# A kernel ordered by its own planner: transfers planned as two first-in first-out queues, hand-over margins changed

## The chip, the cores and the metric

The kernel runs on one core of a Trainium2 chip. The time is device microseconds of that core; the engines are named as the profile names them: PE (matrix multiply, PEld its weight loads), DVE, ACT, POOL, and SP, which here only issues transfers (DMA).

## The reference

```python
# q, k, v: (4, 8, 576, 64); windowed attention, heads 0-3 plain window 32, heads 4-7 dilated by 4
scores = np.where(masks[None], scale * np.matmul(q, k.transpose(0, 1, 3, 2)), -1e9)
attn = softmax(scores)                                   # over the last axis
x = np.matmul(attn, v) -> tokens x heads: (2304, 512)
g = x @ w_gate                                           # 512 -> 1536
x = (g * (1.0 / (1.0 + np.exp(-g))) * (x @ w_val)) @ w_out   # 1536 -> 512
h = x @ w_in                                             # 512 -> 2048
out = (h - np.tanh(h)) @ w2_out                          # 2048 -> 512
```

All in float32. The weights reach the kernel as 64-bit floats, viewed as integers.

## The kernel before, in words

**Work.** 48 attention units (a pair of heads, 192 query rows) come first. The 2304 tokens are six tiles of 384, in three pairs. Layer 1 (gate, value, out) and layer 2 (in, out) go over blocks of 128 hidden columns, one or two blocks to a *turn*: seven turns in layer 1, eight in layer 2, each over the three pairs of tiles. Every matmul product is made of float32r high and low halves. Where a turn has two blocks and a pair of tiles is joined, the four products of a layer's first matrix are made from seven (`seven_up`), with sums of tiles (`sums_x`) and of weights (`sums_w`) made beforehand.

**Names of the steps.** `convert` brings a weight piece: a transfer into one of two staging buffers `st` (L262), then on ACT `rebias` (L265), which waits for the transfer, on DVE `shift`, `low_bits`, `sign` (L269, L273, L278), the last reader of the staging buffer, then the split into halves (ACT L247, DVE L250). In `seven_up` PE makes products (L429), ACT moves partial sums between PSUM banks (`seed` L440, `keep` L466), DVE adds (L469, L472). The second matrix of layer 1 is L610, of layer 2 L630; ACT or DVE take its result to an accumulator tile `acc` (`put`, L574, L570, L572), and a whole `acc` tile is stored, by SP the first time (L593), by POOL with an accumulating transfer later (L595), and fetched back once for the last turn (L558). Sums of tiles that don't stay on the core are stored (L658) and loaded again (L673). PSUM has 8 banks `ps`.

**What sets the order.** Each step is a task with an engine, a duration, a priority, what it depends on and what buffers it takes. `Plan.order` plays the tasks through in a list of events: whenever an engine is free it takes the ready task with the smallest priority number for which buffers are free. A task is ready a margin after the last task it depends on has ended: `NEAR` on the same engine, `FAR` from another one, or the margin `lat` that the earlier task carries. Tasks are then issued in the order of their planned starts, and on the chip each engine runs its own list strictly in that order, SP its transfers as well: one that has to wait holds up all behind it.

A transfer is, in the plan of before, a task of an engine "DMA" with a fixed duration, one after the other, and a fixed margin behind it. An accumulating store is a POOL task and then an empty "DMA" task of 3.8 us.

Of the kernel before, what the change touches and what calls it, by code (L numbers as in the profile page):

```python
# [23 lines left out]
DM = H * D  # L24
# [63 lines left out]


class Task:  # L90
    def __init__(self, n, eng, dur, prio, emit, deps, bufs, gives, lat, port):
        self.lat, self.n, self.eng, self.dur, self.prio, self.emit = lat, n, eng, dur, prio, emit
        self.port = port
        self.deps, self.bufs, self.gives = [d for d in deps if d is not None], list(bufs), gives
        self.then, self.ready, self.start, self.left = [], 0.0, None, len(self.deps)


class Plan:
# [2 lines left out]
    def __init__(self, rings):  # L101
        self.tasks, self.free = [], {r: list(range(n)) for r, n in rings.items()}

    def add(self, eng, dur, prio, emit, deps=(), bufs=(), gives=None, lat=None, port=False):
        t = Task(len(self.tasks), eng, dur, prio, emit, deps, bufs, gives, lat, port)
        for b in t.bufs:
            b.users += 1
        self.tasks.append(t)
        return t

    def order(self):
        for t in self.tasks:
            for d in t.deps:
                d.then.append(t)
        busy = dict.fromkeys(self.ENGINES, 0.0)
        waiting = {e: [t for t in self.tasks if t.eng == e and not t.left] for e in self.ENGINES}
        events, done, now = [], [], 0.0
        port = None, 0.0
        while True:
            moved = True  # L120
            while moved:
                moved = False
                for e in self.ENGINES:
                    if busy[e] > now:
                        continue
                    best = None
                    for t in waiting[e]:
                        if t.ready > now + 1e-9 or (best is not None and (t.prio, t.n) >= (best.prio, best.n)):
                            continue
# [22 lines left out]
            now, _, t = heapq.heappop(events)  # L152
            if t is None:
                continue
            for u in t.then:
                u.left -= 1
                u.ready = max(u.ready, now + (t.lat or (NEAR if u.eng == t.eng else FAR)))
                if not u.left:
                    waiting[u.eng].append(u)
                    heapq.heappush(events, (u.ready, -1, None))  # L160
# [34 lines left out]
def attention_then_two_ffns(ctx, tc, qk, vt, masks, w1, w2, out):  # L195
# [59 lines left out]
    def convert(src, prio, first=False):  # L255
# [33 lines left out]
    def sums_w(c1, c2, prio):  # L289
# [11 lines left out]
        a = plan.add("DVE", 1.4, prio, combine, [d1, d2], [u1, u2], port=True)  # L301
        return split_w(u1, [a], prio), split_w(u2, [a], prio)


# [28 lines left out]
    def attention(b, hp, g, prio, evac_on):  # L333
# [50 lines left out]
        a = add_att("DMA", Q_DMA, prio, lambda: nc.sync.dma_start(out=q(), in_=qk[b, hp, g]), bufs=[q], lat=DMA_FAR)  # L384
        got_v = add_att("DMA", V_DMA, prio, lambda: nc.sync.dma_start(out=v(), in_=vt[b, hp, g]), bufs=[v], lat=DMA_FAR)
# [167 lines left out]
    def add_up(layer, t, pieces, first, last, prio, early=None):  # L553
# [1 line left out]
        at = new_acc()  # L555
        keep = sums[layer - 1][t]
        if last:
            fetched = plan.add("DMA", 2.0, prio - 6.0, lambda: nc.sync.dma_start(out=at(), in_=keep),  # L558
                               [sum_done[t], early or pieces[0][4][0]], [at], lat=5.0)
        puts = []  # L560
        for n, (mm, c0, c1, dur, deps, bufs) in enumerate(pieces):
            ps = new_ps()
# [32 lines left out]
                nc.gpsimd.dma_start(out=keep, in_=at(), accum_op=ALU.add)  # L595

        if first:
            sum_done[t] = plan.add("DMA", 2.1, prio - 5.0, store, puts, [at], lat=5.0)
# [21 lines left out]
    def ffn2_out(ws, ys, t, first, last, prio, end=False, early=None):  # L620
# [17 lines left out]
        if last:  # L638
            at, puts = r
            for (s, c0, c1), a in zip(cuts, puts):  # L640
                def store(s=s, c0=c0, c1=c1):
                    r0 = t * TT + s * P
                    nc.sync.dma_start(out=out[r0:r0 + P, c0:c1], in_=at()[:, s * DM + c0:s * DM + c1])

                plan.add("DMA", 0.75 * (c1 - c0) / DM, -1e6, store, [a], [at])


    seven_x, spilled, fetched_x = {}, {}, {}
# [1 line left out]
    def spill(p, parts, prio):  # L650

        seven_x[p], spilled[p] = parts[:5], []
        for o, done in parts[5:]:
# [6 lines left out]
            spilled[p].append((home, plan.add("DMA", 2.0, prio, store, [done], [o], lat=4.5)))  # L660
        fetched_x.pop(p, None)

    homes = []
# [1 line left out]
    def parts_of(p, again, prio, begun):  # L665

        if not again or p not in fetched_x:
            fetched_x[p] = []
            for home, done in spilled[p]:
                o = new_x()  # L670

                def load(o=o, home=home):
                    nc.sync.dma_start(out=o().bitcast(F32).rearrange("p s k n -> p (s k n)"), in_=home)  # L673

                fetched_x[p].append((o, plan.add("DMA", 2.0, prio, load, [done, begun], [o], lat=4.5)))
        return seven_x[p] + fetched_x[p]

    def halves(r):
# [54 lines left out]
    def load_mask():  # L733
        nc.sync.dma_start(out=mask, in_=masks)

    got_mask = add_att("DMA", 1.0, ATT0 + 0.1, load_mask, lat=DMA_FAR)
    ps_warm = new_ps()

    def warm_up():
# [250 lines left out]
```

## Time and profile before

| | us |
|---|---|
| median of 3 runs (lowest, highest) | 910.91 (909.21, 913.83) |
| time of the profiled execution | 915.47 |
| its span, first to last instruction | 913.7 |
| PE busy in it | 891.1 |
| DVE, ACT busy in it | 657.6, 557.9 |

The profiled execution is one run, 4.56 us above the median; its span is 1.8 us shorter than its time. A matmul's busy time overlaps the next one's, so busy PE says that PE had no gap, not that it ran at its best.

### The profile page before, as it was taken

The page shows a single profiled execution, that of the slowest core. Times are in us where ns is not written, and L with a number is a line of the kernel's source. Part 1 is how long each engine was busy: PE and PEld are TensorE (multiplying, and loading weights), DVE is VectorE, ACT ScalarE, POOL GpSimd, SP SyncE. Part 2 cuts the span into 40 slices and gives each one's busy share as a digit, 9 for nine tenths or more (in the row PEclk, how much of TensorE's full clock was granted, in tenths as well). Part 3 has the DMA queues.
Part 4 walks back from the last instruction along what each step waited for, and adds up shares of the span by engine and source line. Part 5 has one row for each costly group of instructions (what it writes and reads, how often), then busy time and mean ns, then how long its engine had stood idle before and what let it go on. Part 6 is the DMA issues. An engine that isn't in the chain of part 4 may idle for free.

```text
span 913.7 us, 15222 instructions
## 1 busy us (share of the span) xinstructions
PE 891.1 (98%) x5322; PEld 839.5 (92%) x5322; DVE 657.6 (72%) x1573; ACT 557.9 (61%) x1461; POOL 92.4 (10%) x122
## 2 busy tenths in 40 slices
PE   8899999999999999999999999999999999999997
PEld 6789999999999999999999997988899989899986
DVE  4878897985644743753755999997786868775665
ACT  5688875856655654654655876775575656555531
POOL 2232310100000000000000000001010111111100
PEclk7799999999999999999999999999999999999999
DMA  9777844995675685586595566689889797959995
GB/s 277 216 244 259 281 125 121 250 316 151 176 197 105 173 206 106 130 221 168 129 281 178 197 241 253 229 233 236 222 216 239 179 236 188 238 114 228 254 268 219
DMA packets 48086, 189.60 MB, mean 208 GB/s; under 512 B 5504, under 2 KB 10368, under 8 KB 48000
## 3 DMA queue, kind: packets, MB, share of 16 engines
q1 hardware_dynamic: 38496, 136.63, 43.5%
q0 software_dynamic: 9504, 51.91, 31.3%
q8 instruction: 44, 0.72, 0.3%
q14 instruction: 42, 0.34, 0.1%
HBM read 113.02 MB, written 75.50 MB: 206 GB/s over the span
## 4 chain that ended last, share of the span: by engine, by line
PE 86%; DVE 6%; DMA 6%; issue 1%; ACT 1%; SPq 0%; ACTq 0%; DVEq 0%
PE ps L429 37%; PE ps L630 20%; PE ps L610 14%; PE ps L417 8%; PE ps L343 3%; DMA st<-w 3%; PE ps L381 2%; DMA q<-qk 2%; PE ps L368 2%; DVE x L688 1%; DVE y L496 1%; DVE acc L703 1%; DMA x<-part 1%; DVE u L278 0%; DVE wc L250 0%
## 5 line engine op out<-in xcount | busy, mean ns | idle before, releaser
L429 PE MATMUL ps<-x,wc 128*128 128x384 f32 x2184 | 399.5, 336 | 2.5 <-ACT acc L574 1.4
L429 PEld LDWEIGHTS ps<-x,wc 128*128 128x128 f32 x2184 | 383.3, 188 | 8.3 <-ACT ps L440 1.8
L630 PE MATMUL ps<-wc,y 128*128 128x512 f32 (+1 forms) x870 | 207.6, 390 | 0.1
L630 PEld LDWEIGHTS ps<-wc,y 128*128 128x128 f32 x870 | 161.8, 188 | 32.0 <-DVE t L541 0.6
L574 ACT ACTIVATE acc<-ps 128x384 f32<-128x384 f32 (+1 forms) x246 | 125.4, 528 | 91.0 <-PE ps L610 57.5
L610 PE MATMUL ps<-y,wc 128*128 128x384 f32 x864 | 163.4, 338 | 6.0 <-ACT acc L574 6.0
L610 PEld LDWEIGHTS ps<-y,wc 128*128 128x128 f32 x864 | 151.1, 188 | 7.3 <-ACT acc L574 7.3
L595 POOL DMA_DIRECT2D sum<-acc x66 | 57.5, 872 | 679.1 <-ACT acc L574 423.6
L496 DVE TENSOR_TENSOR y<-t,y 128x384 fp32r<-128x384 f32 x168 | 92.5, 555 | 26.7 <-ACT y L493 26.0
L247 ACT ACTIVATE wc<-u 128x512 fp32r<-128x512 f32 x104 | 65.4, 631 | 61.0 <-PE ps L429 43.4
L493 ACT ACTIVATE y<-t 128x384 fp32r<-128x384 f32 x168 | 87.0, 519 | 23.3 <-PE ps L630 12.1
L250 DVE TENSOR_TENSOR wc<-u,wc 128x512 fp32r<-128x512 f32 x104 | 71.7, 694 | 23.2 <-ACT wc L247 22.4
L469 DVE TENSOR_TENSOR ps<-ps,t 128x384 f32<-128x384 f32 x52 | 29.5, 566 | 69.3 <-PE ps L429 69.1
L417 PE MATMUL ps<-x,wc 128*128 128x384 f32 x384 | 72.0, 342 | 0.0
L417 PEld LDWEIGHTS ps<-x,wc 128*128 128x128 f32 x384 | 67.6, 192 | 0.3
L440 ACT ACTIVATE ps<-ps 128x384 f32<-128x384 f32 x104 | 49.7, 478 | 28.1 <-PE ps L429 26.4
L538 DVE SCALAR_TENSOR_TENSOR t<-t 128x384 f32<-128x384 f32 x96 | 53.2, 556 | 12.8 <-ACT t L535 12.4
L354 ACT ACTIVATE e<-e,nm 128x96 f32<-128x96 f32 x144 | 52.2, 371 | 11.3 <-DVE nm L348 11.3
L265 ACT ACTIVATE u<-st 128x512 f32<-128x512 f32 x68 | 45.1, 670 | 22.2 <-DMA st<-w 21.8
L535 ACT ACTIVATE t<-ps 128x384 f32<-128x384 f32 x72 | 35.2, 489 | 31.5 <-DVE ps L469 20.9
L343 PE MATMUL ps<-q 128*128 128x96 f32 x288 | 44.5, 302 | 4.4 <-DMA q<-qk 4.4
L269 DVE TENSOR_SCALAR u<-u 128x512 uint32<-128x512 uint32 x68 | 29.3, 432 | 26.6 <-ACT u L265 26.5
(61 smaller groups left out, 814.8 us busy)
## 6 DMA issues: line engine op xcount, KB each, us to landing
sum<-acc POOLq DMA_DIRECT2D x66, 768.0 KB, 8.4
x<-part SPq DMA_DIRECT2D x58, 768.0 KB, 6.3
st<-w SPq DMA_DIRECT2D x68, 512.0 KB, 5.6
q<-qk SPq DMA_DIRECT2D x48, 304.0 KB, 5.2
sum<-acc SPq DMA_DIRECT2D x12, 768.0 KB, 5.2
part<-x SPq DMA_DIRECT2D x12, 768.0 KB, 4.6
acc<-sum SPq DMA_DIRECT2D x12, 768.0 KB, 6.7
v<-vt SPq DMA_DIRECT2D x48, 144.0 KB, 4.2
```

Source lines behind the costliest of these rows:

```text
L247: nc.scalar.activation(out=w()[:, 0, :], in_=u(), func=AF.Copy)
L250: nc.vector.tensor_tensor(out=w()[:, 1, :], in0=u(), in1=w()[:, 0, :].bitcast(F32), op=ALU.subtract)
L343: nc.tensor.matmul(ps()[:, i * KT:(i + 1) * KT], lhsT=q()[:, i * P:(i + 1) * P], rhs=q()[:, k0:k0 + KT], start=True, stop=True)
L417: nc.tensor.matmul(ps()[:, :TT], lhsT=w()[:, a, kc * P:(kc + 1) * P], rhs=xt[kc // 2]()[:, bb, kc % 2, :], start=(n == 0), stop=(n == 3 * ...
L429: nc.tensor.matmul(ps()[:, :TT], lhsT=w()[:, i, c:c + P], rhs=b()[:, j, k, :], start=(start and n == 0), stop=(n == 5), skip_group_check=True)
L493: nc.scalar.activation(out=y()[:, 0, :], in_=s(), func=AF.Copy)
L496: nc.vector.tensor_tensor(out=y()[:, 1, :], in0=s(), in1=y()[:, 0, :].bitcast(F32), op=ALU.subtract)
L538: nc.vector.scalar_tensor_tensor(out=sq(), in0=sq(), scalar=E0 / E1, in1=sq(), op0=ALU.add, op1=ALU.mult)
L574: nc.scalar.activation(out=o, in_=ps()[:, :c1 - c0], func=AF.Copy)
L595: nc.gpsimd.dma_start(out=keep, in_=at(), accum_op=ALU.add)
L610: nc.tensor.matmul(ps()[:, :TT], lhsT=w[2][0]()[:, a, m * P:(m + 1) * P], rhs=y[0]()[:, bb, :], start=(start and n == 0), stop=(n == 3 * l ...
L630: nc.tensor.matmul(ps()[:, :c1 - c0], lhsT=y[0]()[:, a, s * P:(s + 1) * P], rhs=w[1][0]()[:, bb, c0:c1], start=(n == 0), stop=(n == 3 * le ...
```

## The change

Transfers get two first-in first-out queues in the plan: one for those that SP issues, one for those of POOL. SP is busy for `ISSUE`; the transfer enters its queue `LAUNCH` later; the head of each queue is worked on, alone at full rate, and when both queues have one at the rates of `DMA_SHARE`; it is done `LAND` after its work is used up. What depends on it follows `NEAR` after that in the attention part and `SLACK` after it elsewhere. The margins `FAR`, `FIRST_FAR`, `ATT_FAR`, `QUICK` and the priorities `CONV0` and `HURRY` have new values. No arithmetic, no buffer and no instruction's shape changes; every engine's list is ordered anew.

```diff
-    def add(self, eng, dur, prio, emit, deps=(), bufs=(), gives=None, lat=None, port=False):
+    def add(self, eng, dur, prio, emit, deps=(), bufs=(), gives=None, lat=None, port=False, work=0.0):
...
+    def rates(self, queues):
+        heads = [e for e in queues if queues[e]]
+        return [queues[e] for e in heads], [DMA_SHARE[e] for e in heads] if len(heads) > 1 else [1.0]
...
+        queues, moves = {"DMA": [], "POOL": []}, [0.0]
...
-                    heapq.heappush(events, (busy[e], best.n, best))
+                    heapq.heappush(events, (busy[e], best.n, best, "issued" if best.work else "done"))
...
+            if what == "issued":
+                heapq.heappush(events, (now + LAUNCH, t.n, t, "enter"))
+                continue
+            if what in ("enter", "moved"):
+                heads, rate = self.rates(queues)
+                for q, r in zip(heads, rate):
+                    q[0][0] -= (now - moves[-1]) * r
+                for q in heads:
+                    if q[0][0] < 1e-6:
+                        u = q.pop(0)[1]
+                        heapq.heappush(events, (now + LAND, u.n, u, "done"))
+                if what == "enter":
+                    queues[t.eng].append([t.work, t])
...
-NEAR, FAR = 0.2, 1.1
-FIRST_FAR, ATT_FAR, DMA_FAR = 0.2, 0.8, 1.8
+NEAR, FAR = 0.2, 0.7
+FIRST_FAR, ATT_FAR = 0.3, 0.5
+ISSUE, LAUNCH, LAND = 0.45, 1.1, 0.7
+DMA_SHARE = {"DMA": 0.4, "POOL": 0.6}
...
-CONV0 = -18.6
+CONV0 = -15.0
...
-SUM_DMA = 3.8
-Q_DMA, V_DMA = 1.02, 0.5
-QUICK = 0.6
-HURRY = 60.0
+SLACK = 1.5
+SUM_DMA = 3.9
+Q_DMA, V_DMA = 1.12, 0.5
+QUICK = 0.5
+HURRY = 20.0
...
-        a = plan.add("DMA", 1.5, prio, load, bufs=[st], lat=DMA_FAR if first else 3.0)
+        a = plan.add("DMA", ISSUE, prio, load, bufs=[st], lat=NEAR if first else SLACK, work=1.65)
...
-            a = plan.add("POOL", 0.62, prio - 5.0, store, puts + [sum_done[t]], [at], lat=2.0)
-            sum_done[t] = plan.add("DMA", SUM_DMA, prio - 5.0, lambda: None, [a], [at], lat=4.0)
+            sum_done[t] = plan.add("POOL", 0.62, prio - 5.0, store, puts + [sum_done[t]], [at], work=SUM_DMA)
```

Three places show what this makes of the lists. On ACT, in layer 1, around the `rebias` that runs at 246.5 us in the profile of before (`u<-st` is `rebias`, `ps<-ps` a seed, `t<-ps` a `keep` or the gate's function, `acc<-ps` a `put`); first before, then after the change:

```order
L265 ACTIVATE u0_3393<-st0_3335 128x512
L440 ACTIVATE ps3_3398<-ps2_3373 128x384
L511 ACTIVATE t3_3407<-ps0_3350 128x384
L440 ACTIVATE ps1_3362<-ps6_3370 128x384
L466 ACTIVATE t1_3429<-ps4_3412 128x384
L265 ACTIVATE u3_3438<-st1_3396 128x512
L574 ACTIVATE acc2_3447<-ps5_3421 128x384
L574 ACTIVATE acc2_3447<-ps7_3431 128x384
L574 ACTIVATE acc2_3447<-ps0_3440 128x384
L574 ACTIVATE acc2_3447<-ps5_3449 128x384
```

```order
L291 ACTIVATE u0_3377<-st0_3315 128x512
L492 ACTIVATE t0_3387<-ps2_3364 128x384
L466 ACTIVATE ps0_3397<-ps6_3379 128x384
L537 ACTIVATE t4_3410<-ps5_3353 128x384
L600 ACTIVATE acc0_3424<-ps3_3402 128x384
L600 ACTIVATE acc0_3424<-ps7_3415 128x384
L600 ACTIVATE acc0_3424<-ps5_3426 128x384
L600 ACTIVATE acc0_3424<-ps3_3434 128x384
L466 ACTIVATE ps2_3364<-ps4_3373 128x384
L492 ACTIVATE t5_3464<-ps1_3449 128x384
L291 ACTIVATE u1_3466<-st1_3400 128x512
```

The second `rebias` of the excerpt (from `st1`) stood ahead of the four puts and now stands behind them, a seed and a `keep`. On PE at the same place (L610, now L635, are the matmuls that feed the four puts, six for each; L429, now L455, are products of `seven_up`), before and after:

```order
L429 MATMUL ps6_3370<-x8_2799,wc8_3252 128x384 x6
L429 MATMUL ps4_3412<-x16_2774,wc4_3313 128x384 x6
L610 MATMUL ps5_3421<-y0_3288,wc0_2442 128x384 x3
L610 MATMUL ps5_3421<-y3_3381,wc2_2574 128x384 x3
L610 MATMUL ps7_3431<-y0_3288,wc0_2442 128x384 x3
L610 MATMUL ps7_3431<-y3_3381,wc2_2574 128x384 x3
L610 MATMUL ps0_3440<-y0_3288,wc0_2442 128x384 x3
L610 MATMUL ps0_3440<-y3_3381,wc2_2574 128x384 x3
L610 MATMUL ps5_3449<-y0_3288,wc0_2442 128x384 x3
L610 MATMUL ps5_3449<-y3_3381,wc2_2574 128x384 x3
```

```order
L635 MATMUL ps3_3402<-y0_3278,wc0_2431 128x384 x3
L635 MATMUL ps3_3402<-y5_3371,wc2_2532 128x384 x3
L635 MATMUL ps7_3415<-y0_3278,wc0_2431 128x384 x3
L635 MATMUL ps7_3415<-y5_3371,wc2_2532 128x384 x3
L635 MATMUL ps5_3426<-y0_3278,wc0_2431 128x384 x3
L635 MATMUL ps5_3426<-y5_3371,wc2_2532 128x384 x3
L635 MATMUL ps3_3434<-y0_3278,wc0_2431 128x384 x3
L635 MATMUL ps3_3434<-y5_3371,wc2_2532 128x384 x3
L455 MATMUL ps4_3373<-x8_2762,wc8_3251 128x384 x6
L455 MATMUL ps1_3449<-x16_2728,wc4_3312 128x384 x6
```

The two products that the seed and the `keep` ahead of the second `rebias` wait for stood ahead of the four groups and now stand behind them. The third place is SP's list early in the attention part (`q<-qk` and `v<-vt` load one attention unit each, `st<-w1` the third weight piece; `q` has 6 buffers, `v` 8), before and after:

```order
L384 DMA q5_424<-qk 128x608
L385 DMA v3_437<-vt 96x384
L384 DMA q0_452<-qk 128x608
L262 DMA st0_467<-w1 128x512
L385 DMA v4_494<-vt 96x384
L384 DMA q1_506<-qk 128x608
L385 DMA v5_513<-vt 96x384
L384 DMA q2_528<-qk 128x608
```

```order
L410 DMA q0_300<-qk 128x608
L410 DMA q1_339<-qk 128x608
L411 DMA v3_347<-vt 96x384
L411 DMA v4_365<-vt 96x384
L411 DMA v5_398<-vt 96x384
L410 DMA q2_413<-qk 128x608
L411 DMA v6_427<-vt 96x384
L288 DMA st0_435<-w1 128x512
L410 DMA q3_444<-qk 128x608
```

The third weight piece stood right behind the thirteenth `q` load (`q0`, with which the ring of six is gone through for the third time); two more `q` loads (`q1`, `q2`) and three more `v` loads (`v4` to `v6`) now go ahead of it.

## Rows read from the trace of the kernel before

**Rows 1.** The page's head and its first section.
```profile
span 913.7 us, 15222 instructions
...
PE 891.1 (98%) x5322; PEld 839.5 (92%) x5322; DVE 657.6 (72%) x1573; ACT 557.9 (61%) x1461; POOL 92.4 (10%) x122
```

**Rows 2.** Windows: length, busy PE, PEld, DVE, ACT, POOL; granted clock, DMA, GB/s.
```profile
0.00:25.00 25.00, 21.44 (x157) 16.73 (x157) 12.55 (x90) 14.47 (x72) 5.42 (x15) 0.80 0.96 276
25.00:50.00 25.00, 22.59 (x193) 21.15 (x194) 20.16 (x110) 17.29 (x79) 7.02 (x10) 0.80 0.70 206
50.00:75.00 25.00, 22.90 (x238) 20.20 (x237) 19.39 (x110) 20.67 (x95) 8.44 (x12) 0.93 0.81 260
...
225.00:250.00 25.00, 23.69 (x136) 23.37 (x136) 18.14 (x35) 16.27 (x34) 1.90 (x3) 1.00 0.62 158
...
525.00:550.00 25.00, 24.61 (x134) 23.23 (x133) 25.00 (x41) 18.76 (x44) 0.00 (x0) 1.00 0.59 225
550.00:575.00 25.00, 23.41 (x117) 20.62 (x116) 23.54 (x45) 18.50 (x41) 0.00 (x0) 1.00 0.68 255
```

**Rows 3.** Waits of PE: line, released by what: total us, times, longest.
```profile
PE ps L610 <- ACT acc L574: 6.0, 4, 1.7
PE ps L343 <- DMA q<-qk: 4.4, 5, 2.1
PE ps L429 <- ACT acc L574: 1.4, 1, 1.4
...
PE ps L429 <- ACT ps L440: 1.0, 2, 0.6
```

**Rows 4.** Timeline of ACT, 236 to 250: start, length, what, [idle before].
```profile
243.16 0.49 ACT L466 ACTIVATE t<-ps 128x384 f32<-128x384 f32 x1 [0.53 <-PE ps L429]
246.47 0.66 ACT L265 ACTIVATE u<-st 128x512 f32<-128x512 f32 x1 [2.81 <-DMA st<-w]
247.03 1.24 ACT L574 ACTIVATE acc<-ps 128x384 f32<-128x384 f32 x3
```

**Rows 5.** Timeline of PE, 236 to 250.
```profile
247.56 1.34 PE L610 MATMUL ps<-y,wc 128*128 128x384 f32 x6 [1.31 <-ACT acc L574]
```

**Rows 6.** Chain that ended last, longest pieces: start, length, what.
```profile
239.63 6.75 DMA st<-w
...
452.12 7.17 DMA st<-w
```

**Rows 7.** Transfers of the staging buffers, 225 to 262.
```profile
DMA to landing us min/median/max: 3.5/5.0/7.0
```

**Rows 8.** The page's transfer issues: count, size, us to landing.
```profile
sum<-acc POOLq DMA_DIRECT2D x66, 768.0 KB, 8.4
```

**Rows 9.** Waits of SP's queue, 18 to 32.
```profile
SPq L262 <- DVE u L278: 7.3, 1, 7.3
```

**Rows 10.** Timeline of SP, 20 to 33.
```profile
21.81 0.43 SPq L384 DMA_DIRECT2D q<-qk  x1
29.57 0.33 SPq L262 DMA_DIRECT2D st<-w  x1
...
30.43 0.42 SPq L384 DMA_DIRECT2D q<-qk  x1
```

**Rows 11.** Chain that ended last, first 80 us.
```profile
30.43 4.67 DMA q<-qk
...
40.24 3.42 PE ps L417 x12
...
47.31 2.11 PE ps L417 x12
...
55.57 6.82 DMA q<-qk
```

**Rows 12.** Timeline of all engines, 252 to 256.
```profile
253.54 0.66 ACT L265 ACTIVATE u<-st 128x512 f32<-128x512 f32 x1
...
254.23 0.43 DVE L269 TENSOR_SCALAR u<-u 128x512 uint32<-128x512 uint32 x1 [1.62 <-ACT u L265]
```

More of the change, by code (lines that the diff above doesn't have):

```diff
@@ L90, with __init__ @@
 class Task:
-    def __init__(self, n, eng, dur, prio, emit, deps, bufs, gives, lat, port):
+    def __init__(self, n, eng, dur, prio, emit, deps, bufs, gives, lat, port, work):
         self.lat, self.n, self.eng, self.dur, self.prio, self.emit = lat, n, eng, dur, prio, emit
-        self.port = port
+        self.port, self.work = port, work
         self.deps, self.bufs, self.gives = [d for d in deps if d is not None], list(bufs), gives
@@ L102, in __init__ @@
         self.tasks, self.free = [], {r: list(range(n)) for r, n in rings.items()}
-    def add(self, eng, dur, prio, emit, deps=(), bufs=(), gives=None, lat=None, port=False):
-        t = Task(len(self.tasks), eng, dur, prio, emit, deps, bufs, gives, lat, port)
+    def add(self, eng, dur, prio, emit, deps=(), bufs=(), gives=None, lat=None, port=False, work=0.0):
+        t = Task(len(self.tasks), eng, dur, prio, emit, deps, bufs, gives, lat, port, work)
         for b in t.bufs:
@@ L148, in order @@
                     moved = True
-                    heapq.heappush(events, (busy[e], best.n, best))
+                    heapq.heappush(events, (busy[e], best.n, best, "issued" if best.work else "done"))
             if not events:
                 break
-            now, _, t = heapq.heappop(events)
-            if t is None:
+            now, stamp, t, what = heapq.heappop(events)
+            if what == "wake" or what == "moved" and stamp != -2 - len(moves):
+                continue
+            if what == "issued":
+                heapq.heappush(events, (now + LAUNCH, t.n, t, "enter"))
+                continue
+            if what in ("enter", "moved"):
[8 more added lines that the diff above has]
+                    queues[t.eng].append([t.work, t])
+                moves.append(now)
+                heads, rate = self.rates(queues)
+                if heads:
+                    heapq.heappush(events, (now + min(q[0][0] / r for q, r in zip(heads, rate)), -2 - len(moves), None, "moved"))
                 continue
@@ L159, in order @@
                     waiting[u.eng].append(u)
-                    heapq.heappush(events, (u.ready, -1, None))
+                    heapq.heappush(events, (u.ready, -1, None, "wake"))
             for b in t.bufs:
@@ L299, in combine @@
             tt(out=u1()[:, hi], in0=u1()[:, hi], in1=u1()[:, lo], op=ALU.subtract)
-        a = plan.add("DVE", 1.4, prio, combine, [d1, d2], [u1, u2], port=True)
+        a = plan.add("DVE", 1.2, prio, combine, [d1, d2], [u1, u2], port=True)
         return split_w(u1, [a], prio), split_w(u2, [a], prio)
@@ L382, in mix @@
                                      lhsT=v()[:, c:c + D], rhs=at()[:, c:c + D], start=True, stop=True)
-        a = add_att("DMA", Q_DMA, prio, lambda: nc.sync.dma_start(out=q(), in_=qk[b, hp, g]), bufs=[q], lat=DMA_FAR)
-        got_v = add_att("DMA", V_DMA, prio, lambda: nc.sync.dma_start(out=v(), in_=vt[b, hp, g]), bufs=[v], lat=DMA_FAR)
+        a = add_att("DMA", ISSUE, prio, lambda: nc.sync.dma_start(out=q(), in_=qk[b, hp, g]), bufs=[q], lat=NEAR, work=Q_DMA)
+        got_v = add_att("DMA", ISSUE, prio, lambda: nc.sync.dma_start(out=v(), in_=vt[b, hp, g]), bufs=[v], lat=NEAR, work=V_DMA)
         a = add_att("PE", 0.67, prio, scores, [a], [ps, q])
@@ L557, in add_up @@
         if last:
-            fetched = plan.add("DMA", 2.0, prio - 6.0, lambda: nc.sync.dma_start(out=at(), in_=keep),
-                               [sum_done[t], early or pieces[0][4][0]], [at], lat=5.0)
+            fetched = plan.add("DMA", ISSUE, prio - 6.0, lambda: nc.sync.dma_start(out=at(), in_=keep),
+                               [sum_done[t], early or pieces[0][4][0]], [at], lat=SLACK, work=2.3)
         puts = []
@@ L597, in add_up @@
         if first:
-            sum_done[t] = plan.add("DMA", 2.1, prio - 5.0, store, puts, [at], lat=5.0)
+            sum_done[t] = plan.add("DMA", ISSUE, prio - 5.0, store, puts, [at], work=2.3)
         else:
-            a = plan.add("POOL", 0.62, prio - 5.0, store, puts + [sum_done[t]], [at], lat=2.0)
-            sum_done[t] = plan.add("DMA", SUM_DMA, prio - 5.0, lambda: None, [a], [at], lat=4.0)
+            sum_done[t] = plan.add("POOL", 0.62, prio - 5.0, store, puts + [sum_done[t]], [at], work=SUM_DMA)
     def ffn1_out(ws, ys, t, first, last, prio):
@@ L643, in store @@
                     nc.sync.dma_start(out=out[r0:r0 + P, c0:c1], in_=at()[:, s * DM + c0:s * DM + c1])
-                plan.add("DMA", 0.75 * (c1 - c0) / DM, -1e6, store, [a], [at])
+                plan.add("DMA", ISSUE, -1e6, store, [a], [at], work=0.9 * (c1 - c0) / DM)
     seven_x, spilled, fetched_x = {}, {}, {}
@@ L658, in store @@
                 nc.sync.dma_start(out=home, in_=o().bitcast(F32).rearrange("p s k n -> p (s k n)"))
-            spilled[p].append((home, plan.add("DMA", 2.0, prio, store, [done], [o], lat=4.5)))
+            spilled[p].append((home, plan.add("DMA", ISSUE, prio, store, [done], [o], work=1.85)))
         fetched_x.pop(p, None)
@@ L673, in load @@
                     nc.sync.dma_start(out=o().bitcast(F32).rearrange("p s k n -> p (s k n)"), in_=home)
-                fetched_x[p].append((o, plan.add("DMA", 2.0, prio, load, [done, begun], [o], lat=4.5)))
+                fetched_x[p].append((o, plan.add("DMA", ISSUE, prio, load, [done, begun], [o], lat=SLACK, work=2.15)))
         return seven_x[p] + fetched_x[p]
@@ L734, in load_mask @@
         nc.sync.dma_start(out=mask, in_=masks)
-    got_mask = add_att("DMA", 1.0, ATT0 + 0.1, load_mask, lat=DMA_FAR)
+    got_mask = add_att("DMA", ISSUE, ATT0 + 0.1, load_mask, lat=NEAR, work=1.0)
     ps_warm = new_ps()
```

## Prediction

> **What bounds the kernel now.** I read the page's head, then the windows of 25 us, then what PE waited for, and at each wait the timeline of the engine named and the chain. PE is busy 891.1 of a span of 913.7 us [rows 1]: over most of it PE is the bound, and an order of the lists can only win back the gaps and the time at the lower clock. The windows show where these are. From 0 to 75 us PE is busy 21.44, 22.59 and 22.90 of 25 at a mean granted clock of 0.80, 0.80 and 0.93; later windows stand at a clock of 1.00, and those of them that have a gap look like 225 to 250 (23.69) and 550 to 575 (23.41) [rows 2]. The waits name them: 6.0 us in four stalls on a `put` (L574), 4.4 us on `q` loads, 1.4 and 1.0 us of products on ACT [rows 3].
>
> The four stalls are one pattern, once per turn of layer 1 from 240 us on. ACT ends a `keep` at 243.65, then stands 2.81 us before a `rebias` whose weight piece has not landed, and the puts behind it start only at 247.03 [rows 4]; PE, which has run out of PSUM banks, idles 1.31 us until the first put is done [rows 5]. The piece took 6.75 us from issue to landing, in the last of the four stalls 7.17 [rows 6], while the quickest near by took 3.5 [rows 7]; a POOL store that goes on beside it takes 8.4 by the median [rows 8].
>
> In the attention part SP is the place to look. Between 21.81 and 29.57 it issues nothing [rows 10]: it stands 7.3 us before the third weight piece, whose staging buffer `sign` has not yet freed [rows 9], and the `q` load behind it, issued at 30.43, is on the chain for 4.67 us, another from 55.57 for 6.82 [rows 11].
>
> **Part A, the four stalls.** The order on ACT puts this `rebias` behind the four puts, a seed and a `keep`. The `keep` now waits for a product that PE reaches four groups of six matmuls later. Twelve matmuls of this size take 2.11 us at the full clock [rows 11], so six take 1.05 and four groups 4.2: ACT reaches `rebias` at about 243.65 + 4.2 = 247.8. The piece is issued when `sign` of the piece two before is done, which the DVE list leaves at about the same place, so it lands as before, at 239.63 + 6.75 = 246.4, or 246.8 at the slowest of the four. It is there 1.0 us before ACT asks, and even where it comes late, the puts that PE waited for are done. What is late next: two additions of `seven_up` on DVE behind `shift`; with ACT not waiting, `shift` follows at 248.5, before the products that they add are ready. The order shows the same move in all four turns. I take the whole **-6.0** [rows 3]; between bounds of -6.0 and -3 (half of it back, if POOL's stores slide under the new place).
>
> **Part B, the attention part.** Two more `q` loads and three more `v` loads go ahead of the third weight piece, and the `rebias` that waits for it stands later in ACT's list. SP's stop of 7.3 us therefore has work issued ahead of it, and the thirteenth to fifteenth units don't wait for a load issued at 30.43. The load issued at 55.57 is also drawn forward, and the scores that wait for it stand 15 PE rows later. I take 2.5 of the 4.4 us [rows 3]: the two places on the chain are the larger part, the small waits of the first microseconds stay, since there the DMA engines are busy 0.96 of the time [rows 2]. The clock: the first products of layer 1 take 3.42 us where the same twelve take 2.11 seven microseconds later [rows 11]; if the gap ahead of them is shorter, such a stretch may go. I count 0.5 us and leave the rest to a rival: **-3.0**. Bounds: at best all 4.4 and the low clock of the second and third window, 0.20 and 0.07 of 25 us below full, 6.75 us of clock, together -11; at worst +3, as many new gaps as the three `q` waits that it could not remove, because PE's list now has transposes ahead of scores (the first `turn` stands before the fourth scores) and waits for POOL there.
>
> **Part C, layer 1 to layer 2.** From 525 to 550 DVE is busy all of 25.00 us, then 23.54 [rows 2]; PE waits 1.4 us for a `put`, which ACT holds behind a split of `acc` that waits for DVE, and 0.4 of the 1.0 on seeds lies there [rows 3]. After the change the splits for the last pair stand some eight DVE rows earlier, the conversions of the second turn later, and two puts ahead of the split. **-1.0**; bounds -1.8, and +1.6, what the window at 550 lost before once more [rows 2], since DVE has no room there and the whole piece is shuffled.
>
> **Part D, the end.** The other 0.6 of the 1.0 is a seed at 887 [rows 3]; a group of the last layer stands there now. But a `put` that needs a fetched `acc` now stands on DVE ahead of the two additions. The fetch is issued earlier, too. **-0.5**; bounds -0.6 and +1.
>
> **Part E, thinner margins.** `FAR` goes from 1.1 to 0.7, `QUICK` from 0.6 to 0.5. What a hand-over takes: DVE starts 0.03 us after ACT has ended (253.54 + 0.66 = 254.20, and 254.23) [rows 12]. That leaves room at 0.7, and the dense windows of before show that 1.1 held. In what the durations leave out, some task will still be late: **+1.0**, nearer to nothing than to the other end, by that row. The other end: each of the 38 blocks of `seven_up` pairs (14 in layer 1, 24 in layer 2) loses the 0.4 us by which the margin shrinks, 15.2 us.
>
> The weight, `x` and `acc` loads of layer 2 cost nothing more: the order leaves each load of `x` at least 12 us of PE groups between its free buffer and its product, but for one at 6 in both kernels, and the slowest kind of transfer lands in 8.4 us by the median [rows 8].
>
> **Sum.** -6.0 - 3.0 - 1.0 - 0.5 + 1.0 = -9.5, from 915.47 to 906.0 for a profiled run. That run lies 4.56 above the median of the three, so against the median: 910.91 - 9.5 = 901.4, rounded to **901.5**.
>
> **Rivals.** *The start gives more.* If the two stops of SP were also what let the clock fall, part B gives 4.4 less the early 1.0, and 5 of the 6.75 us of clock: -8.4 in place of -3.0, 896. For it: low clock stands just behind each gap. Against: the first 20 us stay bound by loads. The Trainium skill (TensorE: Matmul & The Clock Gate, section "HAM oscillation — how this bites in real kernels") says that waits between bursts of matmuls put the array back to its half clock, so that a wait costs more than its length; the trace agrees as far as 0.80 and 0.80 in the windows with the `q` waits against 1.00 beside the shorter stalls of layer 1 [rows 2].
>
> *The start gives nothing back.* SP's list is strict, and one stop only moves to another load: part B +3, C 0, the others as above: -2.5, 908.5, within half a per cent. For it: each earlier `q` load means a later weight piece, and layer 1's first products are PE's filler from 40 us on.
>
> *The margins are too thin*, the slower side. One mechanism: in every block a hand-over comes late and PE waits 0.4 us, 15.2 us over 38 blocks in place of 1.0: -9.5 + 14.2 = +4.7, 915.6. It decides from 0.28 us a block (10.5 over 38), at which the gain is gone. For it: PE has no slack of its own to swallow a late task. Against: 0.03 us in the row against 0.7 planned.
>
> **Chances.** Forecast 0.48 (its own range 898 to 906), more at the start 0.20, start lost 0.21, thin margins 0.11. Half a per cent, 4.55 us, is about what a measurement of this kernel can tell from no change: faster is below 906.4, slower above 915.5. Faster 0.68, same 0.22 (the third case, and the thin margins where they cost less), slower 0.10. The range leaves out half of the last case and the far side of the second: 894 to 912.
>
> **What would show it.** A: no wait of PE on L574's `put` with L610 near 240, 310, 381 and 452, and ACT's wait before that `rebias` gone or under 0.5 us with the puts ahead of it. B: SP's longest stop before a weight piece under 3 us in the first 40, the wait of PE on `q` under 2 us, and the granted clock of 25 to 50 above 0.85. C: PE busy over 24 of 25 between 550 and 575. E: no new group of PE waits on DVE or ACT above 2 us in total. I am wrong if PE's gaps in 0 to 75 grow, if the four stalls come back at another `rebias`, or if many waits of 0.2 to 0.5 us appear in layers 1 and 2.

## The result and the profile after

The changed kernel takes 898.19 us (median of 4 runs, 897.42 to 899.14); the kernel before, measured beside it, 911.61 (909.21 to 913.83). The ratio is 0.9854, with an interval of 0.9825 to 0.9883: 13.4 us shorter. Its profiled run took 899.14 us, 16.3 less than the profiled run of before (915.47). The two differences part because the profiled run of before lay 3.9 us above its median and that of after 1.0.

The page's head and its first row, as [rows 1]:

```profile
span 897.1 us, 15238 instructions
...
PE 883.8 (99%) x5322; PEld 834.5 (93%) x5322; DVE 654.5 (73%) x1573; ACT 565.7 (63%) x1461; POOL 94.1 (10%) x122
```

The span is 16.6 us shorter, busy PE 7.3: the rest, 9.3, is time in which PE stood idle. Fewer busy microseconds for the same 5322 matmuls mean that some of them ran quicker. The windows, in the columns of [rows 2], show where:

```profile
0.00:25.00 25.00, 19.99 (x169) 15.42 (x169) 13.30 (x88) 15.30 (x72) 5.44 (x15) 0.86 0.94 283
25.00:50.00 25.00, 23.52 (x248) 21.40 (x242) 22.81 (x133) 21.48 (x98) 8.14 (x11) 0.93 1.02 291
50.00:75.00 25.00, 24.89 (x273) 23.06 (x267) 24.07 (x116) 21.65 (x98) 7.81 (x11) 1.00 0.86 255
225.00:250.00 25.00, 25.00 (x145) 25.00 (x145) 16.48 (x32) 14.41 (x30) 1.77 (x2) 1.00 0.70 184
525.00:550.00 25.00, 25.00 (x126) 22.40 (x125) 24.90 (x44) 19.93 (x43) 0.00 (x0) 1.00 0.64 237
550.00:575.00 25.00, 24.06 (x123) 21.85 (x122) 24.09 (x49) 19.86 (x48) 0.00 (x0) 1.00 0.83 295
```

The granted clock of the first three windows was 0.80, 0.80 and 0.93 before; the DMA engines, 0.70 busy in the second window before, are now busy all through it. Between 225 and 250 PE has no gap left. The waits of PE, as [rows 3], all that the view shows:

```profile
PE ps L394 <- POOL e L388: 2.1, 3, 1.1
PE ps L369 <- DMA q<-qk: 1.9, 1, 1.9
PE ps L766 <- DVE warm L265: 1.2, 1, 1.2
PE ps L407 <- DVE at L398: 1.0, 3, 0.4
PE ps L655 <- DVE t L567: 0.9, 1, 0.9
```

The 6.0 us on `put` (L574, now L600), the 1.4 and the 1.0 us of products on ACT are gone; `q` is down from 4.4 to 1.9 (L343, now L369). New is 0.9 us on DVE in layer 2 (L655), and the transposes (L394) wait 1.0 us more for POOL than before. ACT's timeline at the place of [rows 4]:

```profile
236.14 0.49 ACT L600 ACTIVATE acc<-ps 128x384 f32<-128x384 f32 x1 [0.55 <-PE ps L635]
237.18 0.49 ACT L600 ACTIVATE acc<-ps 128x384 f32<-128x384 f32 x1 [0.55 <-PE ps L635]
238.22 0.49 ACT L600 ACTIVATE acc<-ps 128x384 f32<-128x384 f32 x1 [0.55 <-PE ps L635]
...
240.32 0.49 ACT L492 ACTIVATE t<-ps 128x384 f32<-128x384 f32 x1 [0.53 <-PE ps L455]
240.71 0.66 ACT L291 ACTIVATE u<-st 128x512 f32<-128x512 f32 x1
```

The `rebias` (L291) now runs behind the puts with no idle time ahead of it, where it waited 2.81 us for its piece before; the puts wait only for PE.

At the start, the transfers' own row between 25 and 50 us (tenths of DMA busy time in 40 slices of 0.625 us), first of the kernel before, then of the changed one:

```profile
DMA  9410000038799999999999999999994000682689
```

```profile
DMA  9999999999999999999999999899999999999999
```

In the kernel before, five slices from 26.9 us on and three from 44.4 are empty: there is nothing to transfer, since SP has issued nothing. The first gap is its stop of 7.3 us [rows 9]. In the changed kernel SP's waits before a weight piece (L288), between 18 and 32 us, are these:

```profile
SPq L288 <- DVE x L427: 0.2, 1, 0.2
SPq L288 <- DVE u L304: 0.2, 1, 0.2
```

Up to 80 us the longest of them is 2.4 us.

### The profile page after: what moved, and what is told of

It is laid out like the page before. It is cut to its first block, busy times and chain, and to the rows that moved or that the text cites. A ratio compares the mean times of both kernels' runs of the same rounds, so it can differ in the third digit from the quotient of the medians.

```text
span 897.1 us, 15238 instructions
## 1 busy us (share of the span) xinstructions
PE 883.8 (99%) x5322; PEld 834.5 (93%) x5322; DVE 654.5 (73%) x1573; ACT 565.7 (63%) x1461; POOL 94.1 (10%) x122
## 4 chain that ended last, share of the span: by engine, by line
PE 90%; DVE 7%; DMA 2%; issue 1%; ACT 0%; POOL 0%; SPq 0%; DVEq 0%; POOLq 0%
PE ps L455 39%; PE ps L655 21%; PE ps L635 15%; PE ps L443 8%; PE ps L369 3%; PE ps L407 2%; PE ps L394 2%; DVE x L713 2%; DVE acc L728 1%; DMA q<-qk 1%; DMA x<-part 0%; DMA part<-x 0%; DVE e L374 0%; DVE wc L276 0%; DVE y L522 0%
## 5 line engine op out<-in xcount | busy, mean ns | idle before, releaser
L455 PE MATMUL ps<-x,wc 128*128 128x384 f32 x2184 | 401.4, 336 | 0.0
L455 PEld LDWEIGHTS ps<-x,wc 128*128 128x128 f32 x2184 | 384.0, 188 | 4.9 <-ACT ps L466 0.3
L655 PE MATMUL ps<-wc,y 128*128 128x512 f32 (+1 forms) x870 | 208.1, 390 | 0.9 <-DVE t L567 0.9
L600 ACT ACTIVATE acc<-ps 128x384 f32<-128x384 f32 (+1 forms) x246 | 128.2, 528 | 108.0 <-PE ps L655 54.8
L655 PEld LDWEIGHTS ps<-wc,y 128*128 128x128 f32 x870 | 161.8, 188 | 32.5 <-DVE t L567 1.4
L635 PE MATMUL ps<-y,wc 128*128 128x384 f32 x864 | 164.0, 336 | 0.0
L635 PEld LDWEIGHTS ps<-y,wc 128*128 128x128 f32 x864 | 150.8, 188 | 0.7 <-DVE acc L596 0.3
L522 DVE TENSOR_TENSOR y<-t,y 128x384 fp32r<-128x384 f32 x168 | 92.5, 554 | 10.9 <-ACT y L519 10.1
L276 DVE TENSOR_TENSOR wc<-u,wc 128x512 fp32r<-128x512 f32 x104 | 70.5, 690 | 37.9 <-ACT wc L273 37.1
L548 DVE SCALAR_TENSOR_TENSOR t<-t,ps 128x384 f32<-128x384 f32 x58 | 31.9, 550 | 67.7 <-PE ps L455 39.9
L291 ACT ACTIVATE u<-st 128x512 f32<-128x512 f32 x68 | 45.1, 666 | 6.2 <-DVE wc L276 3.0
L299 DVE SCALAR_TENSOR_TENSOR u<-st,u 128x512 uint32<-128x512 uint32 x68 | 46.6, 685 | 0.7
```

What stands on the lines that cost most here:

```text
L276: nc.vector.tensor_tensor(out=w()[:, 1, :], in0=u(), in1=w()[:, 0, :].bitcast(F32), op=ALU.subtract)
L455: nc.tensor.matmul(ps()[:, :TT], lhsT=w()[:, i, c:c + P], rhs=b()[:, j, k, :], start=(start and n == 0), stop=(n == 5), skip_group_check=True)
L522: nc.vector.tensor_tensor(out=y()[:, 1, :], in0=s(), in1=y()[:, 0, :].bitcast(F32), op=ALU.subtract)
L600: nc.scalar.activation(out=o, in_=ps()[:, :c1 - c0], func=AF.Copy)
L635: nc.tensor.matmul(ps()[:, :TT], lhsT=w[2][0]()[:, a, m * P:(m + 1) * P], rhs=y[0]()[:, bb, :], start=(start and n == 0), stop=(n == 3 * l ...
L655: nc.tensor.matmul(ps()[:, :c1 - c0], lhsT=y[0]()[:, a, s * P:(s + 1) * P], rhs=w[1][0]()[:, bb, c0:c1], start=(n == 0), stop=(n == 3 * le ...
```

## The experiments

Each ratio is to the kernel before, run beside the kernel on the same chip (medians there 913.2 to 914.3 us). The span is that of the profiled run: 913.7 for the kernel before, 897.1 for the changed one.

### 1. The queues without the margins

```diff
 # from the changed kernel
-NEAR, FAR = 0.2, 0.7
-FIRST_FAR, ATT_FAR = 0.3, 0.5
+NEAR, FAR = 0.2, 1.1
+FIRST_FAR, ATT_FAR = 0.2, 0.8
-CONV0 = -15.0
+CONV0 = -18.6
-QUICK = 0.5
-HURRY = 20.0
+QUICK = 0.6
+HURRY = 60.0
```

> The changed kernel with the margins and priorities of before (FAR 1.1, FIRST_FAR 0.2, ATT_FAR 0.8, QUICK 0.6, CONV0 -18.6, HURRY 60): the two transfer queues alone. In its list the rebias of the four stalls stands behind three of the four puts. Theory (the queues make the gain, at the start and in the four stalls): 898 to 903, no PE wait on the puts at 240, 310, 381, 452. Rival (the shorter margins do it): 905 or more, with the start as in before.

909.17 us, ratio 0.9947 (0.9927 to 0.9966), span 907.4. The four stalls stay away and the start is as good as in the changed kernel, but the time is given back from 525 us on. Windows, then PE's longest wait and one near the end, at 890 us:

```profile
525.00:550.00 25.00, 23.13 (x114) 20.09 (x114) 24.93 (x44) 18.43 (x40) 0.00 (x0) 1.00 0.71 262
550.00:575.00 25.00, 21.80 (x106) 19.18 (x104) 20.38 (x42) 16.31 (x39) 0.00 (x0) 0.93 0.61 222
```

```profile
PE ps L655 <- DVE t L567: 3.2, 2, 3.0
...
PE ps L875 <- DVE total L870: 1.5, 1, 1.5
```

PE is busy 4.1 us less than in the changed kernel in these two windows, and the clock falls to 0.93 behind the wait of 3.0 us. The wait at the end, on a count in `total` that PE sums up there, is not in the changed kernel either. So the queues are not the whole gain.

### 2. The margins without the queues

```diff
 # from the kernel before
-NEAR, FAR = 0.2, 1.1
-FIRST_FAR, ATT_FAR, DMA_FAR = 0.2, 0.8, 1.8
+NEAR, FAR = 0.2, 0.7
+FIRST_FAR, ATT_FAR, DMA_FAR = 0.3, 0.5, 1.8
-CONV0 = -18.6
+CONV0 = -15.0
-QUICK = 0.6
-HURRY = 60.0
+QUICK = 0.5
+HURRY = 20.0
```

> The kernel before with the new margins and priorities alone, transfers planned as before. Its list already has the rebias of the four stalls behind three of the four puts. Theory (queues needed): at most the four stalls go, 904 to 907, and the start keeps SP's stop before the third weight piece and PE's loss of about 36 us up to 150 us. Rival (margins do it all): 897 to 901.

908.27 us, ratio 0.9954 (0.9927 to 0.9981), span 904.4. The four old stalls are gone, as the theory allowed. In the profile the start is better too without any queue, which was not expected; but this execution, 906.22 us at a mean granted clock of 0.995, is the quickest of ten, whose medians are 908.27 and 0.991, so part of that start belongs to this one run. And a new stall appears at 197 us. PE's first wait, ACT's wait that lies behind it, the transfer on the chain, and the window after it:

```profile
PE ps L429 <- DVE t L472: 5.2, 2, 4.8
```

```profile
ACT x L685 <- DMA part<-x: 7.1, 1, 7.1
```

```profile
189.78 9.35 DMA part<-x
```

```profile
200.00:225.00 25.00, 22.30 (x119) 22.30 (x120) 11.12 (x21) 12.77 (x28) 1.74 (x2) 0.93 0.57 143
```

A store that spills an `x` tile lands 9.35 us after its issue; a split on ACT (L685), which writes the same buffer, stands behind it in the list, and PE behind that. The old plan frees this buffer when the transfer's fixed 2.0 us are over.

### 3. One margin: 5.0 behind a weight piece

```diff
 # from the kernel before
-        a = plan.add("DMA", 1.5, prio, load, bufs=[st], lat=DMA_FAR if first else 3.0)
+        a = plan.add("DMA", 1.5, prio, load, bufs=[st], lat=DMA_FAR if first else 5.0)
```

> The kernel before with one number changed: the margin behind a weight piece 5.0 in place of 3.0 us (not in the first turn). Part A alone: its list puts the rebias behind two of the four puts. Theory: the four stalls of 6.0 us of PE gaps go for the most part, 904.5 to 907.5, the start as before. Rival (the wait only moves to another place): 909 to 912.

906.23 us, ratio 0.9898 (0.9854 to 0.9943), span 904.1. The window from 225 to 500, first of the kernel before, then of this one:

```profile
225.00:500.00 275.00, 269.02 (x1537) 267.74 (x1537) 152.78 (x287) 153.82 (x322) 19.13 (x22) 1.00 0.67 173
```

```profile
225.00:500.00 275.00, 275.00 (x1580) 275.00 (x1579) 158.23 (x294) 161.88 (x336) 18.33 (x21) 1.00 0.66 173
```

One number moves the four `rebias` and wins the 6.0 us of PE, and by the ratio two thirds of what the whole change gains.

### 4. One margin at the start: 4.5 behind the first turn's pieces

```diff
 # from the kernel before
-        a = plan.add("DMA", 1.5, prio, load, bufs=[st], lat=DMA_FAR if first else 3.0)
+        a = plan.add("DMA", 1.5, prio, load, bufs=[st], lat=4.5 if first else 3.0)
```

> The kernel before with one number changed: the margin behind a weight piece of the first turn 4.5 in place of 1.8 us. Part B in its smallest form: the third weight piece goes two transfers later in SP's list, its rebias ten PE groups behind the freeing of its buffer in place of six; the four stalls stay. Theory (SP's stop before that piece costs the start): 906 to 910, SP's stop shorter, less time at the low clock. Rival (the start is bound by loads anyway): 911 to 913.

916.48 us, ratio 1.0025 (1.0003 to 1.0046), span 913.2: no gain, if anything a small loss. SP's longest stop fell from 7.3 to 4.2 us, and the first three windows have the clock of the changed kernel (0.86, 0.93, 1.00), but in the second the DMA engines are still 0.77 busy, and `q` waits are 5.8 us. The four stalls are there, the last of them longer than before; the timeline of PE and the window:

```profile
458.05 2.22 PE L610 MATMUL ps<-y,wc 128*128 128x384 f32 x6 [1.97 <-ACT acc L574]
```

```profile
450.00:475.00 25.00, 23.03 (x123) 22.71 (x122) 12.34 (x23) 11.40 (x25) 0.97 (x2) 0.93 0.85 237
```

### 5. The changed kernel with the two old priorities

```diff
 # from the changed kernel
-CONV0 = -15.0
+CONV0 = -18.6
-HURRY = 20.0
+HURRY = 60.0
```

> The changed kernel with two priorities of before (CONV0 -18.6, HURRY 60), everything else as changed. The kernel with all margins and both priorities of before lost 11 us against the changed one, between 500 and 575 us and behind 875. Theory (the shorter margins hold these two places): nothing of it comes back here, 897 to 900 us, PE busy over 24 of 25 between 525 and 550. Rival (the priorities hold them): 904 to 909, PE busy about 23 of 25 between 525 and 550 and about 22 between 550 and 575.

898.45 us, ratio 0.9839 (0.978 to 0.9897), span 896.4; PE is busy 24.95 and 24.11 of 25 in the two windows from 525. The priorities are worth nothing that shows.

### 6. The changed kernel with the two old margins outside attention

```diff
 # from the changed kernel
-NEAR, FAR = 0.2, 0.7
+NEAR, FAR = 0.2, 1.1
-QUICK = 0.5
+QUICK = 0.6
```

> The changed kernel with FAR 1.1 and QUICK 0.6 of before, the margins of the attention part and both priorities as changed. The other half of the run above. Theory (margins): the loss is here, 904 to 909 us, a wait of PE on the DVE additions near 549 of 2 to 3 us and low clock behind it. Rival (priorities): 897 to 900. If both runs stay under 901, the loss needed both; if both lose, the two places depend on the order as a whole and on no one number.

909.55 us, ratio 0.9957 (0.9932 to 0.9982), span 908.4. The loss of experiment 1 is here as well (909.17 there), with a wait of 1.3 us on `total` at the end. Windows, then the longer wait:

```profile
525.00:550.00 25.00, 23.12 (x118) 20.52 (x117) 25.00 (x44) 19.73 (x43) 0.00 (x0) 1.00 0.69 252
550.00:575.00 25.00, 22.05 (x105) 19.43 (x104) 20.57 (x42) 15.25 (x35) 0.00 (x0) 0.93 0.65 242
```

```profile
PE ps L655 <- DVE t L567: 3.2, 2, 3.0
```

DVE is full from 525 to 550 in both kernels, so what counts is the order of its rows. Ahead of the group that waits (at 556.05 in this kernel, at 551.59 in the changed one) come three splits of `y` (L522); here they are in this kernel, and then in the changed one:

```profile
548.38 0.55 DVE L522 TENSOR_TENSOR y<-t,y 128x384 fp32r<-128x384 f32 x1
548.85 0.68 DVE L304 SCALAR_TENSOR_TENSOR u<-st,u 128x512 uint32<-128x512 uint32 x1
549.46 0.55 DVE L522 TENSOR_TENSOR y<-t,y 128x384 fp32r<-128x384 f32 x1
549.92 0.68 DVE L299 SCALAR_TENSOR_TENSOR u<-st,u 128x512 uint32<-128x512 uint32 x1
550.53 0.55 DVE L522 TENSOR_TENSOR y<-t,y 128x384 fp32r<-128x384 f32 x1
```

```profile
544.32 1.02 DVE L522 TENSOR_TENSOR y<-t,y 128x384 fp32r<-128x384 f32 x2
545.25 0.56 DVE L495 TENSOR_TENSOR ps<-ps,t 128x384 f32<-128x384 f32 x1
...
546.65 0.56 DVE L522 TENSOR_TENSOR y<-t,y 128x384 fp32r<-128x384 f32 x1
```

All three stand about 4 us later. The rows between them are not the delay: from the first split to the third it is 2.15 us here and 2.33 there. The delay is made ahead of them. What differs are the conversions of weight pieces (L276, L295, L299, L304): from 500 us to the end of PE's wait DVE runs 19 such rows, 11.9 us, in this kernel and 13, 8.2 us, in the changed one. The largest part, first of this kernel, then of the changed one:

```profile
L276 DVE TENSOR_TENSOR wc<-u,wc 128x512 fp32r<-128x512 f32 x7 | 4.8, 681 | 0.0
```

```profile
L276 DVE TENSOR_TENSOR wc<-u,wc 128x512 fp32r<-128x512 f32 x4 | 2.7, 685 | 0.0
```

So with the longer margins more of this filler goes ahead of what PE needs. That a task which becomes ready 0.4 us later in the plan is overtaken by such rows is argued from this place; it was not tried by itself, nor was `FAR` without `QUICK`.

### 7. No margin behind the modelled transfers

```diff
 # from the changed kernel
-SLACK = 1.5
+SLACK = 0.2
```

> The changed kernel with the margin behind weight, x and acc loads (SLACK) taken from 1.5 to 0.2, so that only the modelled queues hold a rebias back. In its list the first of the four rebias, near 240 us, stands ahead of the four puts again, the next two behind them. Theory (where the rebias stands decides): the stall at 240 comes back with 1 to 2 us, those at 310 and 380 do not, PE busy 23.3 to 24.2 of 25 between 225 and 250; 899 to 902 in all. Rival (with the transfers ordered by the queues the piece is there in time wherever the rebias stands): 25.0 of 25 there, 897 to 899.

905.02 us, ratio 0.9911 (0.9883 to 0.9939), span 902.5: neither theory's time. Between 225 and 250 PE is busy 25.00 of 25, although the first of the four `rebias` stands ahead of its puts again: it starts at 232.73 with no idle time of ACT ahead of it, so its piece had landed. The loss is in layer 2, where an `x` load and a weight piece come late. PE's waits, then the transfers on the chain:

```profile
PE ps L455 <- DMA x<-part: 1.9, 1, 1.9
PE ps L455 <- ACT ps L466: 1.8, 1, 1.8
```

```profile
571.55 8.82 DMA x<-part
...
590.19 12.23 DMA st<-w
```

### 8. Only SP's stop at the start

```diff
 # from the kernel before
-        a = plan.add("DMA", 1.5, prio, load, bufs=[st], lat=DMA_FAR if first else 3.0)
+        a = plan.add("DMA", 1.5, prio + (8.0 if first and prio > CONV0 + 3.0 else 0.0), load,
+                     bufs=[st], lat=DMA_FAR if first else 3.0)
```

> The kernel before with one priority changed: the load of the third weight piece is planned 8 us later, so that two more q and three more v loads stand ahead of it on SP, as in the changed kernel. The rest is planned as before; the four stalls stay. Theory (SP's stop before this piece is what starves the scores): that stop falls from 7.3 us to under 4, the wait of PE on q loads from 4.4 to under 3, and the first 75 us get 2.5 to 7 us shorter: 904 to 909. Rival (the stop only moves to another load, and the start is short of loads anyway): 911 to 914.

912.44 us, ratio 0.9986 (0.9957 to 1.0014), span 911.1. SP's stop, two waits of PE, and the second window:

```profile
SPq L262 <- DVE u L278: 2.8, 1, 2.8
```

```profile
PE ps L343 <- DMA q<-qk: 1.9, 3, 0.7
PE ps L343 <- ACT at L374: 1.4, 1, 1.4
```

```profile
25.00:50.00 25.00, 23.38 (x244) 21.94 (x244) 24.03 (x135) 20.77 (x98) 7.82 (x11) 0.93 0.81 240
```

The stop, the wait on `q` and the clock (0.80 to 0.93) improve as the theory says, yet the span falls by 2.6 us only, and the medians can't tell that from nothing. Part of it goes into new waits of PE: the scores now wait 1.4 us for ACT, and the four stalls take 6.6 us in place of 6.0.

### 9. Margins shorter still

```diff
 # from the changed kernel
-NEAR, FAR = 0.2, 0.7
-FIRST_FAR, ATT_FAR = 0.3, 0.5
+NEAR, FAR = 0.2, 0.3
+FIRST_FAR, ATT_FAR = 0.3, 0.2
-QUICK = 0.5
+QUICK = 0.2
```

> The changed kernel with the margins made shorter once more: FAR 0.3, ATT_FAR 0.2, QUICK 0.2 in place of 0.7, 0.5 and 0.5. Theory (a hand-over takes far less than any of these, so that thin margins cost nothing): 896 to 901 us, no new group of waits of PE above 2 us, PE busy over 24 of 25 between 525 and 575. Rival (the changed kernel stands near the edge, and below it tasks come late in every block): 904 to 915, with many waits of 0.2 to 0.5 us in layers 1 and 2.

900.85 us, ratio 0.9861 (0.9834 to 0.9889), span 899.7. PE is busy 25.00 of 25 in both windows from 525 on. No cost from tasks that come late in layers 1 and 2 that the intervals separate, and no gain either; one wait of 1.3 us on a split of `y` stands at 885 us.

### 10. A shorter fitted work

```diff
 # from the changed kernel
-SUM_DMA = 3.9
+SUM_DMA = 2.3
```

> The changed kernel with the planned work of a POOL store to sum (SUM_DMA) taken from 3.9 to 2.3, that of an SP store of the same tile; the other fitted sizes stay. In its list the rebias of the four places still stands behind the puts. Theory (the order of the two queues and the margins carry the gain, not the exact sizes): 897 to 902 us. Rival (the fitted size matters): loads beside POOL stores land later than planned, waits of PE on weight pieces, x or acc loads above 2 us in total, 903 to 908.

901.1 us, ratio 0.9863 (0.9835 to 0.9891), span 900.4. The fitted size of a POOL store could be off by 1.6 us without a loss that the intervals separate.

### 11. Fixed margins, chosen better

```diff
 # from the kernel of experiment 2
-        a = plan.add("DMA", 1.5, prio, load, bufs=[st], lat=DMA_FAR if first else 3.0)
+        a = plan.add("DMA", 1.5, prio, load, bufs=[st], lat=DMA_FAR if first else 5.0)
```

> The kernel before, with no queues: fixed margins as before, but the shorter hand-over margins and both priorities of the change, and 5.0 us behind a weight piece in place of 3.0. Theory (the old model frees a spilled x buffer 2 us after its store is issued, and where such a store takes 9 us beside a POOL store a split on ACT stands before it; this the queues cure, not a margin): the wait near 197 is there again, 3 to 5 us, and 903 to 908 in all. Rival (with well chosen fixed margins no model of the transfers is needed): 897 to 901.

905.01 us, ratio 0.9899 (0.9864 to 0.9934), span 902.9. The wait near 197 us is there again, 2.4 us of PE where 3 to 5 were expected, since ACT stands before the spill; and SP stops at the start. ACT's wait, then SP's:

```profile
ACT x L685 <- DMA part<-x: 3.8, 1, 3.8
```

```profile
SPq L262 <- DVE u L278: 5.6, 1, 5.6
```

So the theory's time holds. On the same chip this kernel is 6.5 us behind that of experiment 12, which equals the changed one, and no run of the two overlaps (901.38 to 905.42, and 896.50 to 899.81); the ratios alone, 0.9899 and 0.9854, have intervals that just overlap. A margin behind the weight pieces touches neither place. How much each of the two carries was not separated; the median of the mean granted clock is 0.989 here and 0.996 there.

### 12. The start of experiment 7, the rest as changed

```diff
 # from the changed kernel
-                    ws[i][c] = convert(..., lead + 2 * c, layer == 1 and k == 0)
+                    ws[i][c] = convert(..., lead + 2 * c, layer == 1 and k <= 3)
```

> The changed kernel, with the margin of 1.5 behind a weight piece left out for the first three turns of layer 1 only. It joins the start of the run without that margin to the rest of the changed kernel. Theory (the margin costs at the start, where every engine waits for loads, and pays from layer 1's last turns on): 894 to 898 us, the first 75 us 2 to 3 us shorter, nothing lost near 600. Rival (the start of that run owes its gain to the clock of one execution): 897.5 to 899.5, the same as the changed kernel.

898.55 us, ratio 0.9833 (0.9802 to 0.9865), span 897.5: the same as the changed kernel, so the rival holds. At 238 us the `rebias` stands ahead of its puts as in experiment 7, and here its piece is late. ACT, then the window:

```profile
238.55 0.67 ACT L291 ACTIVATE u<-st 128x512 f32<-128x512 f32 x1 [2.11 <-DMA st<-w]
239.12 1.23 ACT L600 ACTIVATE acc<-ps 128x384 f32<-128x384 f32 x3
```

```profile
225.00:250.00 25.00, 24.39 (x140) 24.07 (x139) 16.56 (x32) 14.13 (x29) 1.73 (x2) 1.00 0.75 195
```

It is the pattern of [rows 4] in small: two kernels with this order, one with the stall and one without. The place in the list makes the stall possible, the landing decides whether it comes.

## Why the prediction was right, and where not

The time lies in the range, 3.3 us below the forecast, at the very edge of the forecast's own range (898 to 906) and nearer to the 896 of the first rival. By its steps:

**A, the four stalls, -6.0: right.** PE's 6.0 us on `put` are gone, and a single margin that moves the same four `rebias` gives PE 275.00 busy of 275 (experiment 3). Experiment 12 brings one of the four back, 0.6 us of it, by putting the `rebias` ahead.

**B, the attention part, -3.0: right on the `q` waits, too small on the clock.** The wait on `q` fell by 2.5 us, as counted. The term of the clock, 0.5 us, is the one that was mis-sized: what the first three windows lie below the full clock is 11.75 us before (0.20, 0.20 and 0.07 of 25 us) and 5.25 after. What the part is worth in all follows from the rest: 16.3 between the profiled runs less 6.0 (A), 1.0 (C) and 0.5 (D) leaves 8.8; by the medians, 13.4, it leaves 5.9. Both take E at nothing. That is most of the way to the first rival, "the start gives more" (-8.4).

How much of it is the clock can't be read from two executions, since the clock differs between runs of one kernel, and the profiled run of before, with a mean granted clock of 0.985, lies at the low end. In 52 runs of the kernel before, beside the experiments, the mean clock lies between 0.985 and 0.997, and the time goes with it: the median is 915.8 us for the 19 at 0.988 or less and 910.5 for the 7 at 0.994 or more. Counted as (1 - clock) x span, each microsecond of clock below full goes with 0.64 us of time in these runs (a straight line through them): time at the lower clock is in good part lost, but not all. By the medians the kernel before lies 9.1 to 10.0 us below the full clock on the three chips, the changed kernel 4.9. Four to five us of clock, at 0.64, are an estimated 3 us; with the 2.5 us on `q` that is most of the 5.9.

The rival's reason, that SP's two stops let the clock fall, holds in part at most. With the first stop alone cut to 2.8 us (experiment 8) the clock rose in the second and third window of the profile as in the changed kernel (0.93 and 1.00), but over ten runs its median was 0.992, against 0.9895 in the 24 runs of the kernel before beside them, and the median time 1.9 us less, which the interval does not tell from nothing. The median is 0.989 to 0.992 in all six kernels without the queues, the one before among them, and 0.993 to 0.9985 in all eight with them. So the remainder of B goes with the queues, and with a denser stream of loads: in the second window the share of the DMA engines is 0.70 to 0.81 in the kernel before and in experiments 3, 4, 8 and 11, 0.94 in experiment 2, and 1.00 to 1.05 in every kernel with the queues. Which moved load carries it stays open.

**C, layer 1 to 2, -1.0: right.** PE busy from 525 to 575 went from 48.02 [rows 2] to 49.06: the waits of 1.4 and 0.4 us that it named are gone, a new one of 0.9 on DVE stands there.

**D, the end, -0.5: in line, not tested.** The wait of a product on a seed is gone from the list of waits.

**E, thinner margins, +1.0: wrong in sign for the margins outside attention.** The step said that what was planned at 0.7 leaves room, and that some tasks would still be late. The first half holds even at 0.3 (experiment 9), so the rival "the margins are too thin" falls. But a margin is also a delay in the plan: with the queues in place and `FAR` and `QUICK` as before, the kernel loses 1.0% (ratios 0.9957 and 0.9854; 9.4 of 913 us), two thirds of what the change gains. The forecast did not see it, it seems, because its sum started from the kernel before, in whose order the old margins cost little at that place. It came out right since A to D were read off the order that both changes made together.

Queues alone (0.9947) and margins alone (0.9954) each give about half a per cent, together 1.5%: each alone leaves a new stall of 3 to 5 us elsewhere, which the other removes. One margin aimed at the four stalls (experiment 3) gave more than either half, 1.0%.

The second rival, "the start gives nothing back", fell: the wait on `q` and the clock both improved from 0 to 75 us.

## What to carry to other kernels

In a list that is fixed ahead of time, a wait for a transfer stops everything behind it on its engine, so look first at what stands behind each wait and move the waiting row behind work that PE needs sooner; one number did that for 6 us here. A planner's safety margin is not free: 1.1 us in place of 0.7 cost 1.0% here, as far as the lists show because more filler rows went ahead of the work that PE waits for on a full engine, while 0.3 in place of 0.7 cost nothing that shows. Judge a planner by the whole order it makes: either half of these rules, tried alone, gave a third of the gain and put a new stall elsewhere. And before a clock is read from one profile, look at the other runs of the same kernel.

## What the hardware showed that was not expected

The clock did not follow the length of a wait of PE in any simple way. All four stalls of the kernel before, up to 1.7 us long, lie between 225 and 500 us at a granted clock of 1.00. Behind waits of 1.84 us in experiment 7 (at 606 us) and 1.97 us in experiment 4, and behind those of 3.0 and 4.8 us in experiments 1, 2 and 6, the window has 0.93, 1.75 of 25 us below full, as part of it ran at the lower level (1.2 GHz); behind one of 2.2 us in experiment 8 (at 457 us) and one of 2.4 us in experiment 11 it has 1.00. The Trainium skill (TensorE: Matmul & The Clock Gate, section "HAM oscillation — how this bites in real kernels") lets a wait between bursts cost more than its length. Five of these kernels show such a wait; three, the one before and those of experiments 8 and 11, show waits of 1.3 to 2.4 us that cost no clock.

A weight piece of 512 KB took 3.4 us from issue to landing at the quickest in the kernel before and 13.5 at the slowest; the one that held PE up in experiment 7 took 12.23, and the spill store of 768 KB in experiment 2 9.35: more than any fixed margin tried here would cover.
